# Sparse attention into a squared-ReLU layer: constants moved, weight loads regrouped, local V shifted on chip

## The chip, the cores and the metric

The kernel runs on one core of one Trainium2 chip. Its five engines work side by side: TensorE (PE; its weight loads are shown as PEld), VectorE (DVE), ScalarE (ACT), GpSimd (POOL) and SyncE (SP). The metric is the device time of one execution in microseconds, the median of several runs. The profile comes from one profiled execution; its span runs from the first to the last instruction.

## The reference

```
q, k, v: [8, 8, 576, 64] f32     w_in: [512, 2048] f32     w_out: [2048, 512] f32
scores = q @ k.T / 8
rel = pos[:, None] - pos[None, :]
mask = (rel >= 0) & (rel < 32)                       for heads 0 to 3 (local)
mask = (rel >= 0) & (both positions equal mod 32)    for heads 4 to 7 (strided)
attn = softmax(where(mask, scores, -1e9))
x = (attn @ v), transposed to [4608 tokens, 512]
h = x @ w_in;  g = relu(h) ** 2;  out = g @ w_out    [4608, 512] f32
```

## The kernel before

The attention is cut into 32 units of two heads of one batch: unit u is batch u // 4, and of each batch the first two units are local, the other two strided. Its result goes, transposed and in bf16, into four tiles xt (one for each unit of a batch, 128 rows by 4608 tokens). The layer behind it runs over nine chunks of 512 tokens. For each chunk mm1 does 16 groups of four matmuls (ff 0 to 15, L604): weights from w_in_b, data from xt, into a PSUM bank ph. ScalarE takes the Relu into one of four r buffers (L610), and VectorE squares r into g_sb (L611), one group later. Then mm2 does 16 groups of four matmuls (L626) with w_out_b as the moving data.

The order on every engine is written out by hand; nothing reorders it. BATCH0 is a list of steps for batch 0, run before the chunks' groups. PLAN gives for a group number the steps that run ahead of that group. A group is four matmuls, so attention steps lie between mm1 and mm2 groups. An engine's instructions run in the order in which they are issued, and a wait holds up what is behind it. The letters of the steps that matter here:

- `c4kv`: cast of unit 4's k rows, by VectorE (last letter a: ScalarE, g: GpSimd); `T4kv`: its transpose on TensorE; `W1q0v`: transpose of batch 1's strided q rows.
- `S5`: scores, exponential, and (later) the masks on VectorE; `D4.0`: product with V of half a local unit; `F`, `X`: the strided product, the transposes by DMA; `N`, `O`, `E`, `P`: the rest of batch 0 and the first matmuls of mm1.
- `l1k4+5`, `r1q`, `U1`, `V1`, `C2q`, `o0`: loads issued by GpSimd, of local k, strided q rows, strided V, local V of a batch, strided q as tall rows (into q_t), a quarter of w_out. Most of them cast from f32 to bf16 on the way.
- `H0v`: shift_v_local. A local query block of 96 looks at 128 keys: its own 96 and the 32 before. In `vl` each block has 128 partitions, the first 32 being the last 32 keys of the block before. `load_v_local_sw` loads 96 partitions, and the shift copies partitions 96 to 127 of each block to 0 to 31 of the next one; `load_v_local_all` loads all 128 from DRAM. Batch 0 uses the first, the others the second.
- `z`: late_constants, a row of fills and one copy on VectorE.

GpSimd's loads go through eight semaphores in turn (named DMASW0 to DMASW7 in the instructions' waits): a load is issued only when the load eight before it has landed. Before the batch 0 steps the queue holds the first q, k and v loads and then w_in in four loads of 512 columns. `vss` are the V tiles of the strided units, whose middle third is ones; `str_rows_t` (q_t, k_t) have 16 spare rows that are zero. The fills of both are in `z`, on VectorE.

Of the kernel before, what the change touches and what calls it, by code (L numbers as in the profile page):

```python
# [15 lines left out]
FIRST = (0, 2, 3, 1)  # L16
NP = 3
BATCH0 = """
    c0qv c0ka T0qa c1kg w2 T0kv S0 c1qv W0k0a w3 W0q0v W0k1a W0q1v T1qv w2 T1kv S2 S1 H0v D0.0 D0.1 S3
    D1.0 N3 D1.1 N2 E0a O3 O2 E1a w1 P0 P23 P1  # L20
"""
PLAN = """
0: l1q4+5 l1k4+5 z
1: r1q U1
3: o0
4: r1k c4kv V1 c5qv
5: o1 l2k8+9 c4qv U2
6: o2 o3 V2 C2q
7: C2k
10: l2q8+9 W1q0v T4qa T4kv c5ka T5qa  # L30
12: S4
13: T5ka
14: W1q1v B7v
16: W1k0a S5!
17: W1k1a
18: D4.0
19: S6!
# [13 lines left out]
35: T8kv  # L51
37: T9kv
38: T8qv C3k
41: S8!
42: T9qa
44: S9! D8.0
46: D8.1
# [97 lines left out]
def kernel(  # L155
# [9 lines left out]
    nc = tc.nc  # L165
# [13 lines left out]
    SR = 80  # L179
# [22 lines left out]
    def bank(nm):  # L202
        if in_b0[0] and nm == "pt":
            nm = "b0"
        t = banks[nm].pop(0)
        banks[nm].append(t)
        while id(t) in unread:
            run_due(lambda x: x[1] == unread[id(t)])
        return t
# [13 lines left out]
    vss = [singles.tile([SP_, NJ, 3, D], BF16, name=f"vs{i}") for i in range(NV)]  # L223
    str_rows_t = {nm: singles.tile([SR, 4, NJ * D], BF16, name=f"{nm}_t") for nm in "qk"}
# [3 lines left out]
    w_in_b = singles.tile([128, 4, d_ff], BF16)  # L228
    w_out_b = singles.tile([128, 16, d_model], BF16)
# [8 lines left out]
    rv0 = b0[:, n_s:n_s + 8 * S].bitcast(FP32).rearrange("p (u c) -> p u c", u=4)  # L238

    w_in_v = moe_w_in.rearrange("(c p) f -> p c f", p=128)  # L240
    w_out_v = moe_w_out.rearrange("(c p) f -> p c f", p=128)

    units = [(b, p) for b in range(B) for p in range(H // 2)]
    st = {}
# [33 lines left out]
    def cast_qk_local(u, name, copy):  # L278
        s = st[u]
        t = qk_in.tile([QL, 6, 2, D], BF16, name=f"{name}_l")  # L280
        copy(t.rearrange("p j h d -> p h j d"), s[name + "f"].rearrange("p h (j d) -> p h j d", j=6))
        s[name] = t
# [37 lines left out]
    def load_str_tall(b, name):  # L320
        src = q if name == "q" else k
        t = str_rows_t[name]
        nc.gpsimd.dma_start(out=t[0:SP_], in_=src[b, 4:8].rearrange("h (p j) d -> p h (j d)", j=NJ))  # L323
        big[b, name] = t
# [8 lines left out]
    def transpose_local(u):  # L333
        s = st[u]
        for name in "qk":
            if name == "k":
                full = kTl[v_slot(u)]
                dst = full[:, 32:32 + S]
            else:
                full = dst = qkT.tile([128, S], BF16, name="qT")  # L340
            nc.sync.dma_start_transpose(out=dst.rearrange("c (t p) -> c t p", p=QL),
                                        in_=s[name].rearrange("p t h d -> p (t h d)"))
            s[name + "T"] = full

    def v_slot(u):
        b, p = units[u]
        return (b * 2 + p % 2) % NV
# [12 lines left out]
    def load_v_local_sw(b):  # L360
        i = (2 * b) % NV
        t = vl_all[:, i:i + 2]
        nc.gpsimd.dma_start(out=t[32:128, :, :, :, 0:D].rearrange("p u h t d -> p (u h t) d"),
                            in_=v[b, 0:4].rearrange("h (t p) d -> p (h t) d", p=QL))
        for u in range(2):
            st.setdefault(4 * b + u, {})["v"] = t[:, u]

    def shift_v_local(b, copy):
        t = vl_all[:, (2 * b) % NV:(2 * b) % NV + 2].rearrange("p u h t d -> p (u h) t d")
        copy(t[0:32, :, 1:NL, 0:D], t[96:128, :, 0:NL - 1, 0:D])  # L370
# [9 lines left out]
            st.setdefault(4 * b + u, {})["v"] = t[:, u]  # L380

    def load_w_in(i):
        f = slice(512 * i, 512 * (i + 1))
        nc.gpsimd.dma_start(out=w_in_b[:, :, f], in_=w_in_v[:, :, f])

    def load_w_out(i):
        c = slice(4 * i, 4 * (i + 1))
        nc.gpsimd.dma_start(out=w_out_b[:, c, :], in_=w_out_v[:, c, :])

    clock = [0]  # L390
    pending = []
# [1 line left out]
    def later(n, fn, key=None):  # L393
        pending.append((clock[0] + n, key, fn))
# [12 lines left out]
    def step_T(u, name, copy):  # L407
        s = st[u]
        src = s[name].rearrange("p j h d -> p (j h d)")
        pt = bank("pt").bitcast(BF16)[:, 0:S]  # L410
        for j in range(6):
            nc.tensor.transpose(pt[:, QL * j:QL * (j + 1)], src[:, 128 * j:128 * (j + 1)],  # L412
                                ident[0:QL, 0:QL])
        if name == "k":
            full = kTl[v_slot(u)]
            dst = full[:, 32:32 + S]
        else:
            full = dst = qkT.tile([128, S], BF16, name="qT")
        copy(dst.rearrange("c (p j) -> c p j", j=6), pt.rearrange("c (j p) -> c p j", j=6))
        s[name + "T"] = full  # L420
# [175 lines left out]
    def mm1(c, ff, kks=range(4), order=range(4), pool=None):  # L596
        if ff == 0 and c not in gs:
            gs[c] = g_pool.tile([128, 16, 512], BF16, name="g_sb")
        g = gs[c]
        if kks[0] == order[0]:  # L600
            phs[ff] = bank(pool or "ph")
        ph = phs[ff]
        for kk in kks:
            nc.tensor.matmul(ph, w_in_b[:, kk, 128 * ff:128 * (ff + 1)],  # L604
                             xt[kk][:, 512 * c:512 * (c + 1)],
                             start=(kk == order[0]), stop=(kk == order[-1]))
        if kks[-1] != order[-1]:
            return
        r = r_pool.tile([128, 512], BF16, name="r")
        nc.scalar.activation(r, ph, AF.Relu)  # L610
        later(1, lambda: nc.vector.tensor_tensor(g[:, ff, :], r, r, op=ALU.mult))  # L611
# [45 lines left out]
    def warm(n):  # L657
        if n:
            pw = bank("py")
            for _ in range(n):  # L660
                nc.tensor.matmul(pw, idle[:, 0:128], idle, start=True, stop=True)
# [3 lines left out]
    def first_part(kks):  # L665
        in_b0[0] = False
        for ff in range(NP):
            mm1(0, ff, kks, FIRST, None if ff < 2 else "py")

    def run_step(word):  # L670
        op, arg = word[0], word[1:]
        if op == "w":
            warm(int(arg))
        elif op == "c":
            cast_qk_local(int(arg[:-2]), arg[-2], ENG[arg[-1]])
        elif op == "T":
            step_T(int(arg[:-2]), arg[-2], ENG[arg[-1]])
        elif op == "W":
            step_TS(int(arg[0]), arg[1], int(arg[2]), ENG[arg[3]])
        elif op == "S":  # L680
            step_S(int(arg.rstrip("!")), int("!" in arg))
        elif op == "N":
            step_N(int(arg))
        elif op == "O":
            step_O(int(arg))
        elif op == "F":
            step_X(int(arg[:-2]), int(arg[-1]))
        elif op == "D":
            u, part = arg.split(".")
            step_D(int(u), int(part))  # L690
        elif op == "E":
            step_E(int(arg.rstrip("av")), ENG.get(arg[-1]))
        elif op == "P":
            first_part([int(x) for x in arg])
        elif op == "H":
            shift_v_local(int(arg[:-1]), ENG[arg[-1]])
        elif op == "C":
            load_str_tall(int(arg[:-1]), arg[-1])
        elif op == "Q":
            load_qk_rows(int(arg[:-1]), arg[-1])  # L700
        elif op == "X":
            transpose_str(int(arg[:-1]), arg[-1])
        elif op == "Y":
            transpose_local(int(arg))
        elif op == "V":
            load_v_local_all(int(arg))
        elif op == "U":
            load_v_str(int(arg))
        elif op == "B":
            spread_v_str(int(arg[:-1]), ENG[arg[-1]])  # L710
        elif op == "l":
            load_qk_local_sw(int(arg[0]), [int(x) for x in arg[2:].split("+")], arg[1])
        elif op == "r":
            load_str_rows(int(arg[0]), arg[1])
        elif op == "i":
            load_w_in(int(arg))
        elif op == "o":
            load_w_out(int(arg))
        elif op == "z":
            late_constants()  # L720
        else:
            raise ValueError(word)

    def late_constants():
        nc.vector.tensor_copy(mask_all, mask_loc.to_broadcast([128, NL, QL]))
        nc.vector.memset(mask_all[0:32, 0], 0.0)
        for t in str_rows_t.values():
            nc.vector.memset(t[64:SR], 0.0)
        for t in kTl[2:]:
            nc.vector.memset(t[:, 0:32], 0.0)  # L730
        for t in vss:
            nc.vector.memset(t[:, :, 1, :], 1.0)  # L732
        for i, e in enumerate(es):
            if i > 1:
                nc.vector.memset(e[:, 2 * S:1280], 1.0)

    nc.scalar.preload_act_table_set("natural_log_exp_and_others")
    load_qk_hw(0)
# [30 lines left out]
                            NEG, -NEG, op0=ALU.mult, op1=ALU.add)  # L769
    load_qk_local_sw(0, (1,))  # L770
    load_v0()
    for i in range(4):
        load_w_in(i)

    for word in BATCH0.split():
# [72 lines left out]
```

## Time and profile before

| what | us |
|---|---|
| median of three runs (313.01 to 315.76) | 313.23 |
| span of the profiled execution | 309.8 |
| TensorE busy | 297.7 |
| ScalarE busy | 195.6 |
| VectorE busy | 165.1 |
| GpSimd busy | 65.7 |
| granted TensorE clock, mean | 0.999 |

The span is what the engines' rows cover; the runs' times hold some 3.4 us more around it. Busy times are sums over all stages. TensorE's pages must be read stage by stage: of its idle time 3.1 us lie in the first 10 us, 0.8 in 10 to 20 us, 2.0 in 20 to 30, 2.0 in 75 to 100, and the rest in small pieces and at the end. The DMA engines are over 90% busy in nearly all slices of the first 200 us.

### The profile page before, as it was taken

The numbers are of one execution on the slowest core, as the hardware profiler recorded it, in microseconds if no ns is written. First come the engines' busy times: TensorE is split into PE (matmuls) and PEld (weight loads), VectorE is DVE, ScalarE is ACT, GpSimd is POOL, SyncE is SP. The second block draws the span as 40 slices with busy tenths as digits, with TensorE's granted clock in tenths as the row PEclk, the third lists the DMA queues.
The fourth block names the chain that finished last, engine by engine and source line by source line (L and its number), as shares of the span: only waits on it lengthen the run. The fifth ranks groups of instructions, "written<-read, shape, count | busy, mean of one in ns | idle before, by whom it ended". The sixth has DMA issues, their size and how long they took to land.

```text
span 309.8 us, 5985 instructions
## 1 busy us (share of the span) xinstructions
PE 297.7 (96%) x2288; PEld 147.1 (47%) x2288; DVE 165.1 (53%) x388; ACT 195.6 (63%) x421; POOL 65.7 (21%) x90
## 2 busy tenths in 40 slices
PE   7987999999899999999999999999999999999996
PEld 2543555445454444444545454445454544444444
DVE  4568765767647763664367554763586334203400
ACT  3774955876877775675488676865777656316611
POOL 8834422006230026047100740000000000000000
PEclk9999999999999999999999999999999999999999
DMA  8999999997999999799996999711101110010012
GB/s 152 190 204 205 190 197 182 156 156 112 177 161 166 142 124 173 161 118 112 161 205 116 119 176 198 136 24 70 68 2 38 68 70 1 34 68 36 0 67 71
DMA packets 97820, 37.23 MB, mean 120 GB/s; under 512 B 78848, under 2 KB 93312, under 8 KB 97792
## 3 DMA queue, kind: packets, MB, share of 16 engines
q0 software_dynamic: 59136, 18.76, 60.0%
q1 hardware_dynamic: 38512, 18.03, 30.2%
q8 instruction: 18, 0.29, 0.4%
q14 instruction: 10, 0.08, 0.1%
q10 hardware_dynamic: 144, 0.07, 0.1%
HBM read 38.08 MB, written 9.44 MB: 153 GB/s over the span
## 4 chain that ended last, share of the span: by engine, by line
PE 87%; DVE 4%; issue 3%; ACT 3%; DMA 2%; POOL 0%; DVEq 0%; ACTq 0%; POOLq 0%
PE ph L604 39%; PE ph L626 34%; PE pt L452 4%; DMA w_out_b<-in_k_dram 2%; PE pt L562 2%; PE pt L539 2%; DVE xt L567 2%; PE pt L412 1%; PE py L626 1%; PE ph L651 1%; PE pt L626 1%; ACT rv L563 1%; DVE vs L732 1%; ACT rv L564 1%; PE pt L305 1%
## 5 line engine op out<-in xcount | busy, mean ns | idle before, releaser
L604 PE MATMUL ph<-xt,w_in_b 128*128 128x512 bf16 x572 | 132.0, 379 | 3.4 <-ACT r L610 2.6
L626 PE MATMUL ph<-w_out_b,g_sb 128*128 128x512 bf16 x528 | 121.5, 379 | 0.0
L610 ACT ACTIVATE r<-ph 128x512 bf16<-128x512 f32 x143 | 85.4, 599 | 35.1 <-PE ph L604 30.2
L611 DVE TENSOR_TENSOR g_sb<-r 128x512 bf16<-128x512 bf16 x144 | 60.4, 423 | 64.9 <-ACT r L610 63.4
L604 PEld LDWEIGHTS <-w_in_b 128*128 128x128 bf16 x576 | 53.4, 98 | 63.6 <-issue 4.9
L626 PEld LDWEIGHTS <-g_sb 128*128 128x128 bf16 x560 | 51.8, 98 | 56.4
L567 DVE TENSOR_TENSOR xt<-pt,rv 64x288 bf16<-64x288 f32 x56 | 35.9, 642 | 42.0 <-ACT rv L564 40.8
L462 ACT ACTIVATE e<-pt 128x288 bf16<-128x288 f32 (+1 forms) x124 | 44.0, 409 | 13.2 <-PE pt L452 13.1
L630 ACT COPY y<-ph 128x512 f32<-128x512 f32 x33 | 19.3, 584 | 39.7 <-PE ph L626 39.7
L563 ACT ACTIVATE rv<-pt 64x288 f32<-64x288 f32 x56 | 22.7, 405 | 12.6 <-PE pt L562 11.5
L545 DVE TENSOR_TENSOR x_l<-pt,rinv 96x384 bf16<-96x384 f32 x30 | 16.6, 554 | 1.0
L468 DVE TENSOR_TENSOR e<-e,mask_all 128x576 bf16<-128x576 bf16 x28 | 12.7, 453 | 5.5 <-ACT e L462 4.8
L323 POOL DMA_DIRECT2D q_t<-in_q_dram x6 | 4.4, 729 | 51.4 <-DMA qT_s<-q_t 35.2
L468 DVE TENSOR_TENSOR e<-e,mask_str 72x576 bf16<-72x576 bf16 x28 | 12.4, 448 | 3.1 <-ACT e L462 3.1
L562 PEld LDWEIGHTS <-vs 72*128 72x128 bf16 x224 | 10.6, 98 | 6.3 <-DVE xt L567 0.5
L564 ACT ACTIVATE rv<-rv 128x288 f32<-128x288 f32 x28 | 12.4, 442 | 0.9
L378 POOL DMA_DIRECT2D vl<-in_v_dram x7 | 10.1, 1442 | 13.3 <-DMA vl<-in_v_dram 6.4
L562 PE MATMUL pt<-e,vs 72*128 72x72 bf16 x224 | 11.7, 196 | 0.4 <-DVE xt L567 0.4
L262 POOL DMA_DIRECT2D k_l<-in_k_dram x16 | 11.7, 734 | 1.8 <-DMA k_t<-in_k_dram 1.5
L262 POOL DMA_DIRECT2D q_l<-in_q_dram x16 | 11.6, 730 | 1.0 <-issue 0.7
L539 PEld LDWEIGHTS <-e 128*128 128x128 bf16 x192 | 9.0, 98 | 5.7 <-issue 0.4
L323 POOL DMA_DIRECT2D k_t<-in_k_dram x6 | 4.4, 730 | 31.5 <-DMA kT_s<-k_t 30.3
(110 smaller groups left out, 173.9 us busy)
## 6 DMA issues: line engine op xcount, KB each, us to landing
out_dram<-y SPq DMA_DIRECT2D x35, 256.0 KB, 4.1
vl<-in_v_dram POOLq DMA_DIRECT2D x7, 384.0 KB, 13.4
w_in_b<-in_moe_w_in_dram POOLq DMA_DIRECT2D x4, 512.0 KB, 12.1
w_out_b<-in_moe_w_out_dram POOLq DMA_DIRECT2D x4, 512.0 KB, 16.8
v_st<-in_v_dram POOLq DMA_DIRECT2D x7, 288.0 KB, 10.8
q_t<-in_q_dram POOLq DMA_DIRECT2D x6, 288.0 KB, 6.1
k_t<-in_k_dram POOLq DMA_DIRECT2D x6, 288.0 KB, 6.6
xt<-in_q_dram POOLq DMA_DIRECT2D x4, 288.0 KB, 15.3
```

The lines of the kernel that those rows point to most:

```text
L262: nc.gpsimd.dma_start(out=t[:, :, hh, :], in_=src[b, 2 * p + hh].rearrange("(t p) d -> p t d", p=QL))
L462: nc.scalar.activation(e[0:kn, lo:lo + S // 2], pss[row][half][0:kn, 0:S // 2], AF.Exp, scale=scale)
L468: nc.vector.tensor_tensor(x, x, m, op=ALU.mult)
L545: nc.vector.tensor_tensor(x, po[0:QL, :, 0:D], rinv[0:QL].to_broadcast([QL, NL, D]), op=ALU.mult)
L562: nc.tensor.matmul(po[:, SP_ * t:SP_ * (t + 1)], w, e[0:SP_, c:c + SP_], start=True, stop=True)
L563: nc.scalar.activation(rv[64 * h:64 * h + 64], po[64 - 64 * h:128 - 64 * h, 0:hw], AF.Ln)
L567: nc.vector.tensor_tensor(xt[p][r, b * S:(b + 1) * S].rearrange("c (p j r) -> c p j r", j=NJ // 2, r=2)[:, :, :, part], pos[h][r, 0:hw].re ...
L604: nc.tensor.matmul(ph, w_in_b[:, kk, 128 * ff:128 * (ff + 1)], xt[kk][:, 512 * c:512 * (c + 1)], start=(kk == order[0]), stop=(kk == order ...
L610: nc.scalar.activation(r, ph, AF.Relu)
L611: later(1, lambda: nc.vector.tensor_tensor(g[:, ff, :], r, r, op=ALU.mult))
L626: nc.tensor.matmul(py, g[:, ff, 128 * j:128 * (j + 1)], w_out_b[:, ff, :], start=(ff == 0), stop=(ff == 15))
L630: nc.scalar.copy(y, py)
```

## The change

1. The fills of `vss` (ones) leave `z` and become step `m0123` in batch 0, behind `S0`, still on VectorE. The zero fills of q_t and k_t leave `z` and become step `mr` in group 1, behind `U1`, on GpSimd.
2. w_in is loaded in two loads of 1024 columns in place of four of 512.
3. w_out: a load i still takes 512 rows of the matrix into `w_out_b[:, 4i:4i+4, :]`, but partition p now holds the rows 512 i + 4 p + c (four rows that follow one another in DRAM), where it held 512 i + 128 c + p. To match, mm1 takes as weights every fourth column of w_in_b, so that row p of g_sb for ff belongs to that row of w_out.
4. Local V of batches 1 and 2 is loaded with `load_v_local_sw` (steps `v1`, `v2` in place of `V1`, `V2`), and the shift is done on VectorE in the new steps `H1v` (group 16) and `H2v` (group 41). Batches 3 to 7 stay.

```diff
-    c0qv c0ka T0qa c1kg w2 T0kv S0 c1qv W0k0a w3 ...
+    c0qv c0ka T0qa c1kg w2 T0kv S0 m0123 c1qv W0k0a w3 ...
-1: r1q U1
+1: r1q U1 mr
-4: r1k c4kv V1 c5qv
+4: r1k c4kv v1 c5qv
-6: o2 o3 V2 C2q
+6: o2 o3 v2 C2q
-16: W1k0a S5!
+16: W1k0a S5! H1v
-41: S8!
+41: H2v S8!
...
-    w_out_v = moe_w_out.rearrange("(c p) f -> p c f", p=128)
+    w_out_v = moe_w_out.rearrange("(i p c) f -> i p c f", i=4, c=4)
...
     def load_w_in(i):
-        f = slice(512 * i, 512 * (i + 1))
+        f = slice(1024 * i, 1024 * (i + 1))
...
     def load_w_out(i):
-        c = slice(4 * i, 4 * (i + 1))
-        nc.gpsimd.dma_start(out=w_out_b[:, c, :], in_=w_out_v[:, c, :])
+        nc.gpsimd.dma_start(out=w_out_b[:, 4 * i:4 * (i + 1), :], in_=w_out_v[i])
...
+        f0 = 512 * (ff // 4) + ff % 4
         for kk in kks:
-            nc.tensor.matmul(ph, w_in_b[:, kk, 128 * ff:128 * (ff + 1)],
+            nc.tensor.matmul(ph, w_in_b[:, kk, f0:f0 + 509:4],
...
     def late_constants():
...
-        for t in str_rows_t.values():
-            nc.vector.memset(t[64:SR], 0.0)
...
-        for t in vss:
-            nc.vector.memset(t[:, :, 1, :], 1.0)
...
+    def constants(which):
+        if which == "r":
+            for t in str_rows_t.values():
+                nc.gpsimd.memset(t[64:SR], 0.0)
+        else:
+            for i in which:
+                nc.vector.memset(vss[int(i)][:, :, 1, :], 1.0)
...
-    for i in range(4):
+    for i in range(2):
         load_w_in(i)
```

More of the change, by code (lines that the diff above doesn't have):

```diff
@@ L18 @@
 BATCH0 = """
-    c0qv c0ka T0qa c1kg w2 T0kv S0 c1qv W0k0a w3 W0q0v W0k1a W0q1v T1qv w2 T1kv S2 S1 H0v D0.0 D0.1 S3
+    c0qv c0ka T0qa c1kg w2 T0kv S0 m0123 c1qv W0k0a w3 W0q0v W0k1a W0q1v T1qv w2 T1kv S2 S1 H0v D0.0 D0.1 S3
     D1.0 N3 D1.1 N2 E0a O3 O2 E1a w1 P0 P23 P1
@@ L704, in run_step @@
             transpose_local(int(arg))
+        elif op == "v":
+            load_v_local_sw(int(arg))
         elif op == "V":
@@ L718, in run_step @@
             load_w_out(int(arg))
+        elif op == "m":
+            constants(arg)
         elif op == "z":
```

## The prediction

> **What bounds the kernel now.** I read the totals first, then the slices, the chain of work that ended last, the waits, and at last the engines in order of time in the one stage where TensorE stands.
>
> ```profile
> span 309.8 us, 5985 instructions
> PE 297.7 (96%) x2288; PEld 147.1 (47%) x2288; DVE 165.1 (53%) x388; ACT 195.6 (63%) x421; POOL 65.7 (21%) x90
> ...
> PE   7987999999899999999999999999999999999996
> ```
>
> TensorE is busy for 297.7 of 309.8 us; 12.1 us are left to win at most. The fourth slice (23.2 to 31 us) is one of the few below 9. No edit here removes a matmul, so a gain can only come out of such a hole. The chain in order of time, limited to 18 to 45 us, shows what fills it:
>
> ```profile
> 22.72 1.09 ACT r L610 x2
> 23.83 0.43 DVE g_sb L611
> ...
> 24.90 0.91 DVE q_t L728
> ...
> 25.98 0.91 DVE k_t L728
> ...
> 28.73 0.48 DVE vs L732
> 29.21 0.28 DVE e L735 x2
> 29.49 0.29 DVE g_sb L611
> 29.82 0.04 issue
> 29.86 0.61 ACT r L610
> 30.51 1.02 PE ph L604 x4
> ```
>
> These are the constants of late_constants (step z). VectorE is in them from 24.2 to 29.5 us, and the square of ff 3 (g_sb, L611) stands behind them. There are four r buffers: the Relu of ff 7 needs the one which that square frees, and ff 9 needs the PSUM bank which that Relu reads. The waits between 14 and 60 us say the same:
>
> ```profile
> DVE g_sb L611 <- ACT r L610: 5.2, 5, 2.4
> ...
> ACT r L610 <- DVE g_sb L611: 3.2, 2, 2.7
> ...
> PE ph L604 <- ACT r L610: 2.6, 2, 2.3
> ```
>
> The columns are total us, times, longest us: TensorE stands 2.3 us in one piece, from 28.2 to 30.5 us.
>
> **The change part by part.**
>
> *Constants.* Removed from z: two zero fills of q_t and k_t (2 x 0.91 us, with 0.43 us of issue before them) and four fills of vs. z then ends on VectorE at 25.2 us in place of 29.5: 24.9, plus two kTl fills (0.10), plus two e fills (0.28). So the square of ff 3 is done at 25.6 us, the Relu of ff 7 runs at 27.4 us when its matmuls end, and ff 9 starts at 28.2 us without a wait. The 2.3 us are open to be won.
>
> The four vs fills go to batch 0, behind S0. They are these rows; four cost 2.11 us, from 27.10 to 29.21.
>
> ```profile
> 6.49 0.76 DVE L419 COPY kTl<-pt 128x576 bf16<-128x576 bf16 x1 [1.24 <-PE pt L412]
> 9.71 0.36 DVE L281 COPY q_l<-xt 96x768 bf16<-96x768 bf16 x1 [2.46 <-DMA xt<-in_q_dram]
> ...
> 27.10 2.11 DVE L732 MEMSET vs<- 72x512 bf16 x4
> ```
>
> VectorE stands idle for 2.46 us between the first two rows, until q lands. The fills take 7.25 to 9.36 us and leave 0.35 us; cost 0. Without that cover each us would delay the cast c1qv and batch 0 one for one.
>
> The two zero fills go to GpSimd as 16x2048 bf16. Its nearest rows are the fills of 128x128 (0.22 us) and 128x1 (0.10 us): 0.94 ns a column gives 2.0 us each; with no fixed part, 0.22/128 x 2048 = 3.5 us each. I take 2.0, because the constant part shows, so 4.1 us (bound 7.0). They stand behind the v_st load of U1, at 14.1 to 18.1 us, and ahead of the w_out load o0, which goes at 18.1 in place of 17.06 us. What hides this is the depth of the queue: loads issued there land 15 to 17 us later. Loads already issued before the fills keep the DMA engines supplied until U1 lands (14.49 + 16.7 = 31.2 us), so even 7 us cost nothing. Without that backlog, r1k and V1 behind o0 would land late by as much.
>
> *w_in in two loads.* The four loads land, issue plus time to landing, at 16.8, 19.3, 21.8 and 24.6 us: some 2.5 us for each. Half the columns at a time, ff 0 needs the data that landed at 19.3; its first matmul starts at 19.81, after the copy xt (L589) on ScalarE. The first weight load was at 18.9 us and now waits until about 19.4, which leaves 0.4 us. The second load is there at 24.6, and ff 8 starts at 27.2. Cost 0. Two issues fewer (0.76 us each) let GpSimd run ahead; its cast k_l still waits for k, at 10.4 us.
>
> *w_out four rows a partition.* Same bytes in longer runs. o0 to o3 landed at 33.8, 41.2, 46.3 and 49.0 us and are first used at 39.3, 43.9, 48.9 and 53.1. With TensorE earlier by at most 2.3 us all margins stay above zero, the smallest 0.3 us (o1 and o2). I take no gain in rate. Bounds: by stages the DMA engines move 205 GB/s at 20 to 25 us, where w_in lands, which is also the fastest slice of the page, so nothing above; below, the 187 GB/s of 30 to 35 us, 9% down, or 0.9 us on the four w_in loads (14.2 to 24.6 us).
>
> For this layout the weights of L604 are read with a step of four columns, 576 times 98 ns. No row of before has a stepped weight load. Nearest are copies in which both sides are permuted, against plain ones: ScalarE 0.64 (L419) against 0.63 us (L589), VectorE 0.76 against 0.46. That bounds one load by 98 and 162 ns. The chain has 64 matmuls of L604 in 13.81 us, 215.8 ns each, and the load of the next weights lies inside that. Both ends cost 0.
>
> *Local V.* The loads of batches 1 and 2 have 96 rows instead of 128. V1 took 2.45 us of the queue (35.2 to 37.6), so each saves 0.6 us for all that is behind it. Added are two shifts on VectorE, as H0v: 0.49 us each. H1v comes between the masks of units 4 and 5, where VectorE idles 0.72 us (39.8 to 40.5); it waits for V1, there by 37.0, and VectorE comes to it at about 38. Behind it are the masks of unit 5 and D4.0. H2v, step 41, lies among gaps of 0.44 us between squares, and four r buffers let the squares be late by more than one group, 0.86 us. Cost 0; with no cover 2 x 0.49 us.
>
> **Where the stall goes.** Behind the square of ff 3 VectorE has c4kv (L281), which needs the k rows of l1k; they land at 11.92 + 16.4 = 28.3 us. This wait was covered by z and is now bare. The cast ends at 28.7, c5qv at 29.0, the square of ff 4 at 29.4, c4qv at 29.7, the square of ff 5 at 30.0. The Relu of ff 8 runs 29.4 to 30.0, of ff 9 30.0 to 30.6. TensorE ends ff 9 at 29.1, waits for the rows of r1q (12.59 + 16.6 = 29.2) and for c4qv (29.7), transposes, and begins ff 10 at 30.5 where it began at 32.4: 1.9 us. Then ScalarE, whose queue is only 1.5 us ahead, lets ff 12 start at 33.05 against 34.65: 1.6 us. From 30 us on TensorE is nearly gapless, so what is won there is kept. With l1k 0.7 us sooner all 2.3 us are won; I take 1.75, between them.
>
> The profiled span is 309.8 us, and 3.4 us lie around it to the median of 313.23. The sum: 309.8 - 1.75 = 308.05 in the span, 311.5 in the runs.
>
> **The rivals.**
>
> 1. *The wait moves whole to the data.* If l1k lands 1 us later (longer runs at 9% less give 0.9), the squares and ff 10 slip with it: the gain is 0.6, or none where r1k (landing 35.2, used at 36.6 to 38.6) or l2q (56.7, used at 57.9) catch TensorE again. For it: the DMA queue lags 16 us behind. Against it: V and w_out need no more time than before. 312.2 to 313.2 us.
>
> 2. *Slower: the stepped weight load becomes the pitch of mm1.* It decides from 215.8 / 98 = 2.2 times today's time. At 2.5 times, 245 ns, it costs 29 ns x 576 = 17 us: 313.2 - 1.75 + 17 = 328 us, and more beyond. For it: no such load is in the trace. Against it: the two permuted copies, at 1.0 and 1.65. [...]
>
> 3. *GpSimd's fills hold up VectorE* at 14.1 to 18.1 us, where reciprocals and products of batch 0 (L544, L545) are on the chain. If VectorE stood through both, ff 0 would start 3.7 us late; l1k would no longer be late, so 2.3 of it return: 314.6 us. Against it: GpSimd's cast k_l (10.47 to 11.29) beside two VectorE copies that took 0.48 us each, 0.44 alone. [...]
>
> 4. *More is won*: the earlier order also closes TensorE's waits at 84 to 93 us (1.5 and 0.4 us) beside the full 2.3: 4.2 us, 309.0. Those hang on casts and Ln of their own stage, which nothing here moves.
>
> **How the numbers follow.** Forecast 0.63 (310.9 to 311.7); rival 1 0.12; rival 2 0.11; rival 3 0.06; rival 4 0.08. From 310.0 to 315.0 us lies all but rivals 2 and 4. One per cent is 3.1 us, about what a measurement of this kernel, with runs from 313.01 to 315.76, can tell from no change. Faster by more is rival 4 (0.08), slower by more rival 2 (0.11), the rest 0.81.
>
> **What would show it.** Right: no wait of L604 for r near 28 us; VectorE waiting for the l1k rows at about 28.3; ff 10 near 30.5; weight loads of L604 below 200 ns, 64 matmuls in 13.8 us. Wrong: a wait of weights at 19.4 to 20 for w_in; pitch above 216 ns; VectorE rows at 14 to 18 us stretched; H1v waiting for V1.

## The result, and the profile after

The changed kernel takes 315.43 us (median of 20 runs, 314.78 to 316.24), the kernel before, run beside it, 313.17 us. The ratio is 1.0069, 95% interval 1.0047 to 1.0092: slower by 0.7% where 0.6% less was forecast. The profiled execution has a span of 313.3 us, 3.5 more than the one of before.

The first lines of the page of the kernel after:

```profile
span 313.3 us, 5947 instructions
...
PE 296.9 (95%) x2248; PEld 156.1 (50%) x2288; DVE 164.8 (53%) x388; ACT 195.7 (62%) x421; POOL 66.3 (21%) x90
...
PE   6858999999989999999999999999999999999996
...
PEclk9997999999999999999999999999999999999999
```

The third and fourth slices (15.7 to 31.3 us) have 5 and 8 where TensorE had 8 and 7: the third got emptier, and the fourth, where the hole behind the constants was, fuller. But the fourth has a granted clock of 0.7, which the page of before does not have, and a matmul of L604 takes up to 634 ns in this trace, 390 at most in the one of before. The chain of work that ended last, from 12 us on, names what fills the hole:

```profile
8.09 16.52 DMA w_in_b<-in_moe_w_in_dram
24.61 0.05 issue
24.66 1.90 PE ph L604 x4
26.56 0.85 PE py L604 x2
27.41 0.44 PE ph L604
...
28.52 6.20 PE ph L604 x28
```

Four matmuls took 1.90 us from 24.66 on; from 28.52 on 28 take 6.20, which is 0.89 for four. TensorE in order of time shows where it stopped (the bracket is the idle time before, and who ended it):

```profile
20.02 0.59 PE L604 MATMUL ph<-xt,w_in_b 128*128 128x512 bf16 x2 [1.04 <-ACT xt L588]
20.45 0.38 PE L604 MATMUL py<-xt,w_in_b 128*128 128x512 bf16 x1
24.66 0.62 PE L604 MATMUL ph<-xt,w_in_b 128*128 128x512 bf16 x1 [3.83 <-DMA w_in_b<-in_moe_w_in_dram]
```

Three matmuls of mm1 run: kk 0 of ff 0, 1 and 2. The fourth, kk 2 of ff 0, waits for w_in until 24.66 us. Its weights are every fourth of the columns 0 to 511, all of which came with the first load. That one was issued at 7.35 us and took 12.0 us; the second was issued at 8.1 and took 16.5. So the data was there at 19.4 us, and the matmul waited for the load that landed at 24.6. The list of TensorE's instructions in the built program has this wait written into it (Ldweights is a weight load, Matmult a matmul, what they wait for stands in brackets; DMASW6 and DMASW7 are the semaphores of the two loads; rows 425 to 431, some left out):

```
L604 Ldweights w_in_b [waits DVE_49,DMASW6_49]
L604 Matmult ph_94<-xt_123,w_in_b 128x512 [waits Activation_49]
...
L604 Ldweights w_in_b [waits DMASW7_49]
```

In the list of the kernel before, the wait for DMASW7 stands ahead of ff 4, which does read the second load's columns.

Behind the hole the clock is low for a while. By stages (the columns are the stretch, the time busy of PE, PEld, DVE, ACT and POOL, the granted clock, the DMA share and GB/s):

```profile
19.00:24.60 5.60, 0.81 (x3) 0.34 (x3) 1.68 (x3) 1.51 (x3) 1.24 (x2) 1.00 1.18 208
24.60:28.00 3.40, 3.34 (x8) 1.21 (x9) 0.00 (x0) 0.12 (x1) 1.35 (x3) 0.50 1.27 204
28.00:30.50 2.50, 2.37 (x12) 1.16 (x11) 1.81 (x9) 2.10 (x5) 1.19 (x2) 1.00 1.17 216
```

In 3.4 us at a clock of 0.50 TensorE does half of what it could (8 matmuls, where before had 17 in this stretch): 1.7 us are lost beside the 3.8 us of the hole. The mean clock of this execution is 0.995; 17 of the 20 runs have 0.987 to 0.989, so their low stretch is about twice as long, some 6.9 us (an estimate: 0.011 x 313.5 x 2, at the 0.50 of this trace). They are only 0.3 us slower in the median; where their second half lies, no trace shows. On the other side, the hole behind the constants, 2.3 us before, is gone: no wait of L604 for r near 28 us is in this trace.

### The profile page after: what moved, and what is told of

The parts are those of the page before. It is cut to its first block, busy times and chain, and to the rows that moved or that the text cites. A ratio compares the mean times of both kernels' runs of the same rounds, so it can differ in the third digit from the quotient of the medians.

```text
span 313.3 us, 5947 instructions
## 1 busy us (share of the span) xinstructions
PE 296.9 (95%) x2248; PEld 156.1 (50%) x2288; DVE 164.8 (53%) x388; ACT 195.7 (62%) x421; POOL 66.3 (21%) x90
## 4 chain that ended last, share of the span: by engine, by line
PE 85%; DMA 5%; issue 3%; DVE 2%; POOL 2%; ACT 2%; DVEq 0%; POOLq 0%
PE ph L604 40%; PE ph L626 33%; DMA w_in_b<-in_moe_w_in_dram 5%; PE pt L451 3%; PE pt L561 2%; PE pt L538 2%; DVE xt L566 2%; PE py L626 1%; PE ph L651 1%; PE pt L411 1%; PE pt L626 1%; ACT rv L562 1%; ACT rv L563 1%; POOL xt L274 0%; POOL vl L363 0%
## 5 line engine op out<-in xcount | busy, mean ns | idle before, releaser
L604 PE MATMUL ph<-xt,w_in_b 128*128 128x512 bf16 x554 | 132.4, 382 | 5.9 <-DMA w_in_b<-in_moe_w_in_dram 3.8
L626 PE MATMUL ph<-w_out_b,g_sb 128*128 128x512 bf16 x508 | 119.4, 379 | 1.1 <-issue 0.2
L604 PEld LDWEIGHTS <-w_in_b 128*128 128x128 bf16 x576 | 62.3, 114 | 58.6 <-DMA w_in_b<-in_moe_w_in_dram 4.8
L544 DVE TENSOR_TENSOR x_l<-pt,rinv 96x384 bf16<-96x384 f32 x30 | 16.6, 554 | 1.0
L538 PE MATMUL pt<-vl,e 128*128 128x65 bf16 x180 | 9.9, 194 | 0.0
```

The lines of the kernel that those rows point to most:

```text
L538: nc.tensor.matmul(po[:, n, :], e[:, c:c + 128], rhs[:, NL * part + n, 0:D + 1], start=True, stop=True)
L604: nc.tensor.matmul(ph, w_in_b[:, kk, f0:f0 + 509:4], xt[kk][:, 512 * c:512 * (c + 1)], start=(kk == order[0]), stop=(kk == order[-1]))
L626: nc.tensor.matmul(py, g[:, ff, 128 * j:128 * (j + 1)], w_out_b[:, ff, :], start=(ff == 0), stop=(ff == 15))
```

## The experiments

Three theories were set against each other. A: the new wait is for a load that the matmul does not read, and it and the low clock behind it are the loss. B: the stepped weight loads cost the time. C: w_in in longer runs comes late. Each kernel was run beside the kernel before on the same chip. The changed kernel was not run again there; its 315.43 us come from the result above, where the kernel before had 313.17.

**Two tiles for w_in.** Edit on the changed kernel:

```diff
-    w_in_b = singles.tile([128, 4, d_ff], BF16)
+    w_in_h = [singles.tile([128, 4, d_ff // 2], BF16, name=f"w_in_b{i}") for i in range(2)]
...
-        nc.gpsimd.dma_start(out=w_in_b[:, :, f], in_=w_in_v[:, :, f])
+        nc.gpsimd.dma_start(out=w_in_h[i], in_=w_in_v[:, :, f])
...
-        f0 = 512 * (ff // 4) + ff % 4
+        f0 = 512 * (ff // 4 % 2) + ff % 4
...
-            nc.tensor.matmul(ph, w_in_b[:, kk, f0:f0 + 509:4],
+            nc.tensor.matmul(ph, w_in_h[ff // 8][:, kk, f0:f0 + 509:4],
```

> The changed kernel with w_in in two SBUF tiles of 1024 columns, one for each load; all else as changed. Theory A (a wait for the wrong load): in the changed kernel the fourth weight load of mm1 (ff 0, kk 2) waits for the second w_in load, which it does not read, because a read with a step of four columns and a strided write into one tile are taken to overlap; with two tiles that wait is gone, TensorE has no hole from 20.7 to 24.7 us, the granted clock stays at 1.00, ff 10 begins near 30.5 us, and the time is 311 to 312 us. Theory B (the stepped weight loads, 114 ns against 98, cost the time): it stays near 315. Theory C (w_in in longer runs comes late): TensorE still stands until 24.6 us in ff 0 to 7, and it stays near 315.

Measured: 309.87 us against 313.26, ratio 0.9904 (0.9866 to 0.9942). That is 5.6 us below the changed kernel (5.2 by the ratios to before), with the same loads, the same steps and the same bytes; only the wait is gone. TensorE's waits between 14 and 60 us in the profiled execution, all of them:

```profile
PE ph L604 <- ACT xt L588: 0.8, 1, 0.8
PE pt L561 <- DVE xt L566: 0.4, 1, 0.4
PE ph L604 <- ACT r L610: 0.3, 1, 0.3
```

This execution is the slowest of the six (312.18 us): its matmuls run at half pace until 10.8 us at least (two of 512 columns take 1.05 us at 5.78 us, 0.60 in the trace before at 5.57; one takes 634 ns at 10.8 us, 377 in the trace after at 11.2), where those of before do so until 4.9 (eight in 3.60 us from 1.26 on), though its row of the granted clock says 1.00. So mm1 begins at 22.49 us, some 2.5 us later than in the other traces. Even so kk 2 of ff 0 runs by 23.30 us, and in the trace after the second load landed only at 24.6. B falls as the main cause, and C with it, since ff 0 to 7 wait for no second load; the next kernel, whose mm1 begins at 20.01 us and whose matmuls wait for xt and not for w_in, shows the same for C. The time also went below the 311 to 312 us that A had said.

**No step.** The changed kernel with w_out and mm1's weight columns as before:

```diff
-    w_out_v = moe_w_out.rearrange("(i p c) f -> i p c f", i=4, c=4)
+    w_out_v = moe_w_out.rearrange("(c p) f -> p c f", p=128)
...
-            nc.tensor.matmul(ph, w_in_b[:, kk, f0:f0 + 509:4],
+            nc.tensor.matmul(ph, w_in_b[:, kk, 128 * ff:128 * (ff + 1)],
```

> The changed kernel with w_out and the weight columns of mm1 as before (no step); two w_in loads into one tile, constants and local V as changed. Theory A: no wrong wait either, 311 to 312 us, equal to the two-tile kernel within 0.5 us. Theory B: this kernel alone gains, and is 2 us or more below the two-tile kernel. Theory C: both stay near 315.

Measured: 309.61 us, ratio 0.9893 (0.9855 to 0.9931). One tile, two loads, contiguous columns: no wrong wait either. 0.26 us below the two-tile kernel, inside the bound for A. So the wait needs both, the step and the shared tile. In the built programs of both kernels the wait for the second load stands ahead of ff 8, the first that reads it.

**TensorE kept busy through the hole.** The changed kernel, with this ahead of the fourth matmul (result unused):

```diff
     def first_part(kks):
         in_b0[0] = False
+        if kks[0] == 2:
+            pw = bank("pt")
+            for _ in range(19):
+                nc.tensor.matmul(pw, idle[:, 0:128], idle, start=True, stop=True)
```

> The changed kernel with 19 extra matmuls on zeros (into a free PSUM bank, result unused) between the first three matmuls of mm1 and the fourth, so that TensorE is busy while it would stand. If the granted clock of 0.70 in 25 to 30 us and the 430 ns pitch after the hole come from the hole, then the clock is 1.00 there, the nine matmuls after it take 216 ns each, and the time is 1.9 us below the changed kernel, near 313.5 us; the hole itself stays. If the slow matmuls come from the stepped weight loads, the pitch of 430 ns stays, and so does the time, 315.4 us.

Measured: 313.62 us, ratio to before 1.0024 (0.9998 to 1.0051). The wait is still in the program, and the kernel is 1.8 us faster than the changed one for 19 matmuls more. By stages, in the same stretches:

```profile
19.00:24.60 5.60, 4.78 (x23) 2.31 (x23) 1.55 (x3) 1.38 (x3) 1.23 (x2) 1.00 1.17 209
24.60:28.00 3.40, 3.15 (x15) 1.59 (x14) 0.90 (x3) 1.57 (x3) 1.49 (x3) 1.00 1.28 204
```

The clock stays at 1.00 (a mean of 0.999 or 1.0 in 11 of the 12 runs), and 15 matmuls fit where there were 8. The extra matmuls end 0.14 us after the wait would have (mm1 goes on at 24.80 us and not 24.66), which counts here as hole. So the loss against the two-tile kernel divides into the low clock, 315.43 - 313.62 = 1.8 us, and the hole, 313.62 - 309.87 = 3.75 us.

**Step alone, one tile.** The kernel before with only the layout of w_out and the stepped columns:

```diff
-            nc.tensor.matmul(ph, w_in_b[:, kk, 128 * ff:128 * (ff + 1)],
+            nc.tensor.matmul(ph, w_in_b[:, kk, 512 * (ff // 4) + ff % 4:512 * (ff // 4) + ff % 4 + 509:4],
```

> The kernel before with only the new layout of w_out and the stepped weight columns; four w_in loads into one tile, constants in z, V from DRAM. Theory A: the fourth weight load of mm1 waits for the last of the four loads, until 24.6 us, and the clock falls: 3.8 + 1.9 us lost; the hole behind the constants (2.3 us) stays: 318 to 319 us, the slowest of all. Theory B: 9 us of longer weight loads count only where they are bare; 315 to 316 us without a hole at 20.7 us. Theory C: 313 us, since the w_in loads are those of before.

Measured: 317.45 us, ratio 1.0135 (1.0099 to 1.0171), the slowest of all. Its fourth weight load waits for all three later loads at once:

```
L603 Ldweights w_in_b [waits DMASW7_49,DMASW1_49,DMASW0_49]
```

TensorE stood for 4.0 us, the clock fell to 0.50, and the hole behind the constants was there again, though 1.4 us long and not 2.3. The forecast of 318 to 319 had added the whole wait to 313.2 us, in which a low clock behind the second hole is contained (shown further down); here none followed that hole (1.00 from 31 to 45 us). Counted from the 311.8 us of before's runs at full clock it is 311.8 + 4.0 - 0.9 = 314.9 us. The other 2.55 us fit the half clock behind the first hole, which lasts from 24.7 to about 30.4 us here (0.50 up to 28 us, 0.53 from 28 to 30.5) and can cost up to 2.9 (an estimate: half of 5.7). That the second hole is shorter because TensorE came to it late, at half clock, is argued and not tested.

**Step alone, four tiles.** As the last kernel, with one tile for each of the four loads:

```diff
-    w_in_b = singles.tile([128, 4, d_ff], BF16)
+    w_in_h = [singles.tile([128, 4, d_ff // 4], BF16, name=f"w_in_b{i}") for i in range(4)]
...
-            nc.tensor.matmul(ph, w_in_b[:, kk, 128 * ff:128 * (ff + 1)],
+            nc.tensor.matmul(ph, w_in_h[ff // 4][:, kk, ff % 4:ff % 4 + 509:4],
```

> The kernel before with the new layout of w_out and the stepped weight columns, w_in in four tiles, one for each of its four loads; constants and V as before. It differs from the one-tile kernel of the same layout (317.45 us) only in the tiles. Theory A: no wait for a load that isn't read, no hole at 20.7 us; weight loads of 114 ns stay inside the 216 ns of a matmul, so the time is that of before, 313.2 us within 0.7. Rival (stepped loads cost something of their own): 314.5 us or more.

Measured: 313.50 us against 313.20, ratio 1.0006 (0.9976 to 1.0037). The step and the longer w_out runs cost nothing of their own that can be measured (the interval is -0.8 to 1.2 us), and bring nothing. The groups of weight loads, of the kernel before and then of the changed one, carry the only trace of the step:

```profile
L604 PEld LDWEIGHTS <-w_in_b 128*128 128x128 bf16 x576 | 53.4, 98 | 63.6 <-issue 4.9
```

```profile
L604 PEld LDWEIGHTS <-w_in_b 128*128 128x128 bf16 x576 | 62.3, 114 | 58.6 <-DMA w_in_b<-in_moe_w_in_dram 4.8 <-issue 3.5
```

A load takes 114 ns for 98, and 576 of them 8.9 us more; at 313.50 us against 313.20, all of it lies beside the matmuls.

**The constants alone.** The kernel before with steps m0123 and mr (the part of the change's diff that touches BATCH0, group 1, late_constants and constants).

> The kernel before with only the constants moved (the fills of vs into batch 0, those of q_t and k_t to GpSimd). By the steps of the prediction the hole of 2.3 us goes and the l1k rows take 0.4 to 0.7 of it back: 311.3 to 311.8 us. If the constants are the whole gain of the two-tile kernel, 309.9 us; if they are none of it, 313.2.

Measured: 309.86 us, ratio 0.9903 (0.9866 to 0.994). The constants are the whole gain: the two-tile kernel, which has the rest of the change without the wrong wait, has 309.87. The hole went completely: ff 10 begins at 30.04 us where it began at 32.39. VectorE did wait for the l1k rows, as forecast:

```profile
25.00 0.35 DVE L611 TENSOR_TENSOR g_sb<-r 128x512 bf16<-128x512 bf16 x1
27.45 0.36 DVE L281 COPY k_l<-xt 96x768 bf16<-96x768 bf16 x1 [2.10 <-DMA xt<-in_k_dram]
...
27.99 0.41 DVE L611 TENSOR_TENSOR g_sb<-r 128x512 bf16<-128x512 bf16 x1
```

They landed at 27.4 us and not at 28.3, soon enough for the Relu of ff 8.

**Local V alone.** The kernel before with v1, v2, H1v and H2v in place of V1 and V2.

> The kernel before with only local V of batches 1 and 2 loaded as 96 partitions and shifted on VectorE. By the prediction its cost is hidden, and 0.6 us less of the queue for each changes nothing that TensorE waits for: 313.2 us within 0.5. Rival: the shifts hold up the squares, 314 us; or what the queue saves moves later transfers, and it gains 0.5 us or more.

Measured: 313.44 us against 313.20, ratio 1.0008 (0.998 to 1.0037). Hidden, and worth nothing.

**Two loads alone.** The kernel before with w_in in two loads, one tile, no step.

> The kernel before with only w_in in two loads of 1024 columns, in one tile and with contiguous weight columns. By the prediction the first load lands at about 19.4 us, before it is used, and the time is 313.2 us within 0.5. Rival: the semaphore turns that fall forward by two let GpSimd issue later loads sooner, and it gains 0.5 us or more.

Measured: 313.28 us against 313.20, ratio 1.0006 (0.9969 to 1.0043). Nothing either way.

**The hole of before, filled.** Moving the constants gave 3.3 us in the median, and the hole has only 2.3. The kernel before with ten extra matmuls in the hole (result unused):

```diff
+        if n == 9:
+            pw = bank("pt")
+            for _ in range(10):
+                nc.tensor.matmul(pw, ident, xt[0][:, 0:512], start=True, stop=True)
         g()
```

> The kernel before with ten extra matmuls of 512 columns (2.16 us, into a free PSUM bank, result unused) ahead of ff 9, where TensorE stands for 2.3 us behind the constants. Nothing is taken from the hole's length. Runs of before fall in two groups: granted clock 0.999 or 1.0 with spans of 309.6 to 310.4 us, and 0.993 to 0.995 with 311.2 to 312.2 us. If the hole itself brings on the low clock, all runs here have 0.999 or 1.0, spans near 310 us and a median near 311.8, 1.4 us below before, with more work in the kernel. If the two groups have another cause, both stay and the median is 313.2 us or above.

Measured: 311.78 us, all 12 runs between 311.40 and 312.15 and all at a clock of 1.0. Beside it the kernel before had ten runs at 0.999 or 1.0 (311.68 to 312.23) and seven at 0.993 to 0.995 (313.10 to 315.98), median 312.06; the ratio is 0.9967 (0.9938 to 0.9995). The interval is wide because the groups mix differently each time: beside the earlier kernels, 12 of 17 and 20 of 29 runs of before were in the low group. The spread, not the median, shows the cause: with the hole filled the low group is gone. By stages, in the hole and behind it:

```profile
28.00:30.50 2.50, 2.50 (x13) 1.16 (x12) 2.38 (x8) 0.27 (x1) 1.39 (x2) 1.00 1.25 206
30.50:34.00 3.50, 3.36 (x36) 1.99 (x34) 3.50 (x10) 2.99 (x6) 0.75 (x1) 1.00 1.58 190
```

**Only the fills of vs moved.** The kernel before with step m0123 alone; q_t and k_t stay in z.

> The kernel before with only the four fills of vs moved into batch 0; those of q_t and k_t stay in step z on VectorE. z then ends 2.1 us sooner, at 27.3 us, the square of ff 3 at 27.7, and the Relu of ff 7 runs 0.3 us later than its matmuls allow: a hole of 0.2 to 0.4 us, too short for the low clock. 309.9 to 310.4 us, nearly all of what moving both sets gives (309.86). If each set of fills gives its share of the gain by its length, 311.7 us.

Measured: 309.41 us, ratio 0.9888 (0.9835 to 0.994); lower than forecast by half a microsecond, and as good as both sets. The square of ff 3 is done at 27.7 us, the Relu of ff 7 starts 0.3 us late, and TensorE loses 0.3 us there, as forecast (28 matmuls of mm1 take 6.51 us, 6.20 with both sets moved). All six runs have a clock of 1.0. This kernel and the one without the step (309.61) both beat the kernel before and the changed one by more than their intervals.

## Why the prediction was wrong, step by step

*The step that failed* is "w_in in two loads", with "Cost 0", together with the layout of w_out, "Both ends cost 0". The landing was right: the first load was there at 19.4 us and the first weight load ran at 19.42. In place of that 0 the runs showed 3.75 us of waiting and 1.8 us of low clock behind it. What was left out is the waits that are put into the program when it is built. With the step and one tile, the read of kk 2 is made to wait for the second load, of which it reads no column. The kernels with one tile and a step (315.43 and 317.45 us) have the wait, those without a step or with a tile for each load do not: shown. That the reason is a coarse bound around a stepped read against a load that strides over four kk is only argued. It fits that kk 0, which lies ahead of all the second load's columns in a partition, was let through. Among its signs of being wrong the prediction had a wait of weights for w_in, but at 19.4 to 20 us and for data that come late. It went through the moved instructions and their data, but not through TensorE's new waits, which stand in the list of the changed program.

*The term that was mis-sized* is the hole behind the constants: 1.75 us forecast, 2.3 measured in the spans (309.8 to 307.5), and 3.3 in the medians. The discount for the l1k rows was not paid, as they came 0.9 us earlier. The other 1.0 us is the low clock that the hole brings on in most runs (39 of the 63 beside the experiments), which the profiled execution of before happened not to have. The prediction also put 3.4 us "around" the span; runs with both numbers have 1.7 to 2.0 (315.16 with a span of 313.3, 309.33 with 307.5). The missing 1.5 us was for the most part this low clock in the median: 309.8 + 1.8 is 311.6 us, and none of the three runs (313.01 to 315.76) is as short, which could have been seen.

*The sum*, then: 313.2 - 3.3 (constants) + 3.75 (wrong wait) + 1.8 (clock behind it) = 315.4 us, with V, two loads and layout at 0. The two losses are differences of measured kernels; the trace after, with 3.83 us of hole and 1.7 us lost at half clock, agrees with them.

*Right*: the cover of m0123 (7.28 to 9.39 us, c1qv at 9.92, ended by q's landing and not by the fills), the two fills on GpSimd at 14.29 to 17.83, 1.80 us each against 2.0 (rival 3 did not come: L544 kept its 0.55 us), H1v in a gap at 43.1, the margins of w_out. *Rival 2*, slower by the stepped load, had the right edit and the right sign but the wrong mechanism: the load grew by 1.16 times (98 to 114 ns), far from its 2.2, and the pitch stayed: the last chunk's mm1, 64 matmuls, runs from 282.61 to 296.43 us in the trace after, 13.82 us, against 13.81 before. *Rival 1* did not come either: with two loads the l1k rows landed at 27.1 to 28.3 us (12.14 + 15.5 = 27.6 in the trace after), never later than the 28.3 of before. *Rival 4* had more gain, but by waits at 84 to 93 us that stayed: TensorE is busy for 23.06 of the 25 us from 75 to 100 us in the kernel without the step, 23.05 before.

## What to carry to other kernels

When an edit changes the shape of an access (a step, a permuted view), list the waits of the changed program on the engine that bounds it and compare them with the ones before, row by row; here a wait for a transfer that isn't read cost 3.75 us, and 1.8 of low clock behind it. Loads that are meant to be used one by one go into tiles of their own (309.87 us here, 315.43 in one tile). And price a hole in TensorE at its length plus the half clock behind it: here 2.3 us cost 1.9 to 2.5 us in runs at full clock and 3.5 to 4 in the others, and 3.8 us cost 5.6.

## What the runs showed of the hardware that was not expected

Behind a hole of 2.3 us the clock fell in most runs. Of the 63 runs of the kernel before beside the experiments, 39 have a mean clock of 0.995 or less (312.9 us and more), the others 0.999 or 1.0 (311.4 to 312.2). A profile of the second kind is the one of before; one of the first kind is that of the step in four tiles, which has the same hole:

```profile
28.00:30.50 2.50, 0.38 (x2) 0.11 (x1) 2.39 (x9) 0.47 (x1) 1.33 (x2) 1.00 1.16 212
30.50:34.00 3.50, 3.31 (x29) 2.56 (x30) 3.38 (x9) 2.68 (x6) 0.55 (x1) 0.66 1.56 187
34.00:35.00 1.00, 0.79 (x2) 0.30 (x2) 0.00 (x0) 0.54 (x2) 0.59 (x1) 0.50 1.97 186
```

Here the clock of 1.00 still stands in the hole, and the half clock comes 1 us after work has begun again: 3.5 x 0.34 x 2 = 2.4 us of half clock up to 34 us and 1.0 more from there, 3.4 together. With the hole filled by matmuls, all 12 runs kept the full clock. Behind the 4.0 us hole of the step in one tile the low stretch was about twice as long: 0.85, 0.50 and 0.96 in the stages 20 to 25, 25 to 30 and 30 to 35 us make 6.9 us at 0.50. Why the same hole of 2.3 us brought the low clock in 39 of 63 runs and not in the other 24 no run shows. Of the five runs of before at 315 us and more, two have a mean clock of 0.989, so a low stretch about twice as long (an estimate: 0.011 below full against 0.005 to 0.007); three have 0.995, like the runs at 313 us. For these a late start like that of the two-tile trace, 2.5 us, would fit, but no trace of such a run of before was kept.
